# One core, attention gated with a state-space layer: the gate's store, the size of the state-product steps, the rule for zero products, and the order of head and tail

## The chip, the cores and the metric

The kernel runs on one core of one Trainium2 chip. The metric is the device time of one execution in microseconds (us); the times given are medians of several runs. TensorE (PE) multiplies matrices into PSUM, VectorE (DVE) and ScalarE (ACT) work element by element, GpSimd (POOL) does a few fills here, and SyncE (SP) issues nearly all DMA transfers, in the order of its own queue.

## The reference

x is 2048 x 512 in bf16. Two branches read it, and a gate mixes them:

```python
g = sigmoid((x * gate_w).sum(-1, keepdims=True))
qkv = (x @ wqkv)                       # 32 heads of 16
p = softmax(q @ k.T * 16 ** -0.5)      # per head, 2048 x 2048
a = (p @ v) @ wo
dt = exp(log_dt); logdA = dt * (A_re + 1j * A_im); dB = dt * (B_re + 1j * B_im)
K = einsum("dn,dnl,dn->dl", C, exp(logdA * l), dB).real    # l = 0 .. 2047, N = 128
b = causal_convolution(x, K) + x * Dskip                   # per channel, by FFT
out = g * a + (1 - g) * b
```

The attention has 32 x 2048 x 2048 exponentials. The convolution is computed in the kernel as a chunked recurrence: chunks of 64 positions, a state per channel carried from chunk to chunk by a scan, and inside each chunk a triangular product.

## The kernel before

**Attention.** The work is cut into 2048 tiles: 32 blocks (a query range of 512 and eight heads taken in two halves) by 16 key ranges of 128 by 4 heads of a block. A tile is 128 keys by 512 queries. Four tiles of one block and key range make a quad. Tiles go through in 683 groups of three. For each group TensorE makes the scores (`qk`, line 886) into one of two PSUM buffers SC0 and SC1, ScalarE takes the exponential of the whole group in one instruction (`ex`, line 901, recorded at line 905) into a ring ET of 15 slots, and `pv` (line 932) multiplies a quad of ET by V into the PSUM buffer OA. After the 16 quads of a block VectorE transposes OA (`norm_a`, line 974), divides by the sums (`norm_b`) and transposes back (`norm_c`). Score products of group g + 1 need the buffer that the exponential of group g - 1 has read.

**Tiles on VectorE.** Some groups give one of their three tiles to VectorE, which replaces the exponential by integer arithmetic on bf16 bits: `bits` (line 937) writes a tile of DZ, and when four tiles of a set are there, `batch` (line 947) makes two shifted variants (line 952) and TensorE adds three products per tile, against V and two scaled copies VS0 and VS1 of V. ScalarE's exponential of such a group covers two tiles. Which groups do so is decided in `decide` (line 795): a window of group numbers (`WIN`: first, last, number of buffers, how many sets of keys) must allow it, a buffer must be free, and VectorE's idle time, as the plan counts it, must have grown by a threshold `DVQ` that depends on the stage reached (the last S block, the first scan, the second scan done).

**State-space branch.** VectorE computes the parameters, then tables of powers (`table`, line 1204, into PT); PT is stored to DRAM by SyncE (line 1237) and read back transposed as Qt and as Py. From Qt and blocks of x TensorE makes the S products: `sstage` (line 1281), 16 blocks of four banks of 16 matmuls of 64 x 128 x 32, evicted by VectorE (line 1302). Two scans on VectorE (line 1310) of 30 steps each carry the states. `ystage` (line 1377) then makes 32 units of outputs, scaled by 1 - g from the tile gt, sent to DRAM and read back transposed as Yl. `kstage` (line 1258) makes the kernel inside a chunk. S, K and y products, projections, gate and output rows all share one PSUM bank, MB, under a lock.

**Gate.** `gate` (line 1455) makes 64 small products once all projections are done, an exponential on ScalarE, and then g and 1 - g as 128 x 16 floats, where row p and column i stand for position 128 i + p. They are needed in two other orders (gq and gt), so both are written to DRAM (lines 1479 and 1481) with the position running fastest, that is, as single floats, and read back by eight DMAs (lines 1485 and 1487).

**Order.** All engines' instruction streams are written out ahead by a planner in the same file. Each piece of work is a thread that yields (engine, cost, priority) and then records instructions; `Sched.fill` (line 367) runs, after each group, those threads that can start before the planned end of the exponential, on TensorE up to `OVER` past it. Costs are constants given with each instruction (`c=`). The planned costs fix only the order; on the chip the engines wait on semaphores.

**Zero products.** To keep TensorE's clock up, the planner adds products of zeros (`zero`, line 880). Work is counted in columns of a full 128 x 128 product of 512 (`a=`). After each group it asks for `FILL` columns per 1.335 us of planned ScalarE time, plus what was lacking before, less what was done, and fills up with zeros into OA or MB. `REST` and `FILL2` exist, but with the values given they do nothing.

**Head and tail.** Before the first group (from line 1612) x is transposed on TensorE and copied to xT, the first projections are made, and ScalarE takes exp(log_dt) and two sines, with the loads of its function tables between. After the last group (from line 1714) four groups of output products (a product with the identity that adds Yl, and four with Wo) go to MB and three banks of an SC buffer; the first three products with Wo can be made before the last block is normalised, the fourth needs it. Two copies on ScalarE and two on VectorE, and four stores end the kernel. Every instruction on TensorE is recorded in the helper `mm` (line 622), so all of them carry line 624.

## Time and profile before

| | us |
|---|---|
| median of 3 runs | 855.75 (854.38 to 861.9) |
| profiled execution, whole | 854.42 |
| its span, first to last instruction | 852.6 |
| ScalarE busy | 829.1 |
| VectorE busy | 775.1 |
| TensorE busy | 750.6 |
| exponentials (line 905), busy | 820.8 |

TensorE's mean granted clock is 0.994 of full speed. "Busy" is the time in which at least one instruction of an engine runs; matmuls and exponentials overlap their neighbours, so the distance from one to the next is shorter than a duration. In the rows of groups, the columns are line, engine, operation, output and inputs by name, shape, count; then busy time and the mean of one in ns; then the engine's idle time before them and what ended it. A name with a q (SPq, ACTq) is an engine's queue that issues DMAs. In tables of stretches each row has start and end, then the time, then busy time and count of TensorE, its weight loads, VectorE, ScalarE and GpSimd, then the granted clock, the DMA engines' share and GB/s. A chain row has start, time and what it was.

### The profile page before, as it was taken

How to read it: one execution, taken by the hardware profiler on the slowest of the kernel's cores; microseconds unless marked ns; L12 is line 12 of the kernel's file. 1: busy time of each engine (PE TensorE's matmuls, PEld its weight loads, DVE VectorE, ACT ScalarE, POOL GpSimd, SP SyncE). 2: the span in 40 equal slices, each digit the busy share in tenths (PEclk: the TensorE clock that was granted, in tenths of full speed). 3: DMA queues.
4: the chain of work that ended last, by engine and by line, in shares of the span. 5: the costliest groups of instructions: out<-in, count | busy, mean ns of one | idle time of the engine just before them, and what ended most of it. 6: DMA issues, size and time to landing. Idle time of an engine off the chain costs nothing.

```text
span 852.6 us, 23406 instructions
## 1 busy us (share of the span) xinstructions
PE 750.6 (88%) x10256; PEld 294.3 (35%) x10256; DVE 775.1 (91%) x1313; ACT 829.1 (97%) x695; POOL 11.0 (1%) x13
## 2 busy tenths in 40 slices
PE   7888888878758999999999999988889889999986
PEld 3232332222212443434442445334343233343322
DVE  5799999999959999998899999999999988997985
ACT  7999999999979999999999999999999999999995
POOL 4000000000000000000000000000000000000000
PEclk9999999999989999999999999999999999999999
DMA  9400102942733386558481568016575325454113
GB/s 204 121 2 10 35 4 103 172 153 95 60 129 149 61 191 174 87 146 142 72 109 21 103 100 150 2 49 142 149 160 140 102 88 121 102 137 116 31 35 100
DMA packets 209526, 86.66 MB, mean 102 GB/s; under 512 B 184208, under 2 KB 196368, under 8 KB 207376
## 3 DMA queue, kind: packets, MB, share of 16 engines
q1 hardware_dynamic: 207408, 83.99, 44.9%
q8 instruction: 80, 1.31, 0.6%
q10 hardware_dynamic: 2016, 1.18, 0.6%
q14 instruction: 22, 0.18, 0.1%
HBM read 35.17 MB, written 30.82 MB: 77 GB/s over the span
## 4 chain that ended last, share of the span: by engine, by line
ACT 78%; PE 18%; DMA 2%; DVE 1%; ACTq 0%; issue 0%; SPq 0%; DVEq 0%
ACT ET L905 78%; PE OA L624 7%; PE SC L624 6%; PE MB L624 6%; DMA gm_ptd<-PT 1%; DMA Wq<-in_A_wqkv_dram 1%; DVE tt L999 0%; ACTq L628 0%; DVE Kst L1270 0%; DVE OT L976 0%; ACT fo L1741 0%; DVE KT L714 0%; DVE PT L999 0%; DVE DZ L941 0%; ACT e L1074 0%
## 5 line engine op out<-in xcount | busy, mean ns | idle before, releaser
L905 ACT ACTIVATE ET<-SC 128x1536 bf16<-128x1536 f32 (+1 forms) x683 | 820.8, 1512 | 10.0 <-PE SC L624 9.3
L624 PE MATMUL SC<-Qm,KT 32*128 32x512 bf16 x2048 | 274.7, 385 | 78.1 <-ACT ET L905 63.7
L624 PE MATMUL OA<-wm 128*32 128x512 bf16 (+3 forms) x2136 | 248.0, 339 | 1.2 <-DVE wm L677 1.2
L624 PE MATMUL OA<-ET,VE 128*32 128x512 bf16 x1812 | 181.3, 392 | 6.5 <-DVE OT L976 6.0
L941 DVE TENSOR_SCALAR DZ<-SC 128x512 uint16<-128x512 f32 x236 | 157.4, 685 | 17.0 <-PE SC L624 15.3
L624 PEld LDWEIGHTS SC<-Qm,KT 32*128 32x128 bf16 x2048 | 70.6, 91 | 291.7 <-ACT ET L905 240.4
L624 PEld LDWEIGHTS OA<-ET,VE 128*32 128x32 bf16 x1812 | 46.3, 93 | 108.8 <-issue 99.3
L624 PEld LDWEIGHTS OA<-wm 128*32 128x32 bf16 (+2 forms) x2136 | 71.4, 95 | 32.8 <-issue 16.1
L624 PE MATMUL MB<-X,Qt 64*128 64x32 bf16 x1024 | 74.8, 231 | 0.0
L624 PEld LDWEIGHTS MB<-X,Qt 64*128 64x128 bf16 x1024 | 57.7, 109 | 25.3 <-issue 23.2
L1302 DVE TENSOR_SCALAR SG<-MB 128x512 bf16<-128x512 f32 x64 | 44.0, 688 | 7.8 <-PE MB L624 6.7
L952 DVE TENSOR_SCALAR DZ<-DZ 128x2048 uint16<-128x2048 uint16 x59 | 40.6, 688 | 8.4 <-PE OA L624 8.3
L1337 DVE TENSOR_TENSOR G<-s,s 128x512 f32<-128x512 f32 x60 | 41.3, 688 | 1.1
L1329 DVE TENSOR_TENSOR s<-G,MU 128x512 f32<-128x512 f32 x60 | 41.0, 684 | 0.0
L1334 DVE TENSOR_TENSOR s<-s,SG 128x512 f32<-128x512 f32 x60 | 41.0, 683 | 0.0
L1331 DVE TENSOR_TENSOR s<-G,MU 128x512 f32<-128x512 f32 x60 | 41.0, 683 | 0.0
L952 DVE TENSOR_SCALAR DU<-DZ 128x2048 uint16<-128x2048 uint16 x59 | 40.4, 688 | 0.6
L999 DVE TENSOR_TENSOR ft<-FP,L 128x1024 f32<-128x1024 f32 (+1 forms) x32 | 34.4, 1084 | 0.1
L999 DVE TENSOR_TENSOR PT<-tt,tt 128x1024 bf16<-128x1024 bf16 x48 | 32.9, 685 | 0.7
L624 PEld LDWEIGHTS MB<-Py,SG 128*32 128x32 bf16 x1024 | 29.6, 165 | 7.4 <-issue 4.1
L624 PE MATMUL MB<-Py,SG 128*32 128x64 bf16 x1024 | 30.1, 229 | 0.0
L976 DVE STREAM_TRANSPOSE OT<-OA 128x512 f32<-128x512 f32 x32 | 22.8, 711 | 4.2 <-PE OA L624 3.6
(166 smaller groups left out, 618.2 us busy)
## 6 DMA issues: line engine op xcount, KB each, us to landing
gm_ptd<-PT SPq DMA_DIRECT2D x16, 1024.0 KB, 5.9
Py<-gm_ptd SPq DMA_DIRECT2D x32, 512.0 KB, 4.4
gm_kpd<-Kst SPq DMA_DIRECT2D x16, 256.0 KB, 3.7
Tt<-gm_kpd SPq DMA_DIRECT2D x128, 32.0 KB, 3.4
gm_xrd<-in_A_x_dram SPq DMA_DIRECT2D x1, 2048.0 KB, 13.2
X<-gm_xrd SPq DMA_DIRECT2D x8, 256.0 KB, 4.7
Wo<-in_A_wo_dram SPq DMA_DIRECT2D x4, 512.0 KB, 4.1
XY<-gm_xrd SPq DMA_DIRECT2D x8, 256.0 KB, 4.2
```

Source lines behind the costliest of these rows:

```text
L624: op("PE", lambda t: t.matmul(out(), lhsT(), rhs(), start=start, stop=stop, skip_group_check=True, **kw), R, W, c=c, lat=.15, a=a, cfg=cfg)
L905: op("ACT", lambda a: a.activation(ET(512 * e, [[1, 512 * n]]), sc(0, [[1, 512 * n]]), AF.Exp, scale=DH ** -0.5), [(sc, i, g) for i in ran ...
L941: op("DVE", lambda v: v.tensor_scalar(z.u16(512 * k, [[1, 512 * n]]), sc(512 * na, [[1, 512 * n]]), XS, XB, ALU.mult, ALU.add), [(sc, na + ...
L952: op("DVE", lambda v: v.tensor_scalar(t.u16(0, [[1, 2048]]), z.u16(0, [[1, 2048]]), float(STEP[k][0]), None, ALU.add), R, W, c=.07 + 2048 ...
L976: op("DVE", lambda v: v.transpose(OT(512 * w, [[1, 512]]), OA(0, [[1, 512]])), [(OA, 0, b)], [(OT, w, b)], c=.64)
L999: op(eng, lambda v: v.tensor_tensor(o(), a(), b_(), f), R, W, c=c)
L1302: op("DVE", lambda v, bank=bank, par=par, part=part: v.tensor_scalar(sg(2 * SGH + SGH * part + CB * k8 + 16 * par, [[2 * SGH, 32], [1, 16] ...
L1329: op(e, lambda v: v.tensor_tensor(s2(0, W), G(0, W), MU(d0, [[0, 2], [1, 256]]), ALU.mult), key("G", "MU"), [(s2, 0)], c=F5)
L1331: op(e, lambda v: v.tensor_tensor(s3(0, W), G(256, [[-256, 2], [1, 256]]), MU(D + d0, [[D, 2], [1, 256]]), ALU.mult), key("G", "MU") + [(M ...
L1334: op(e, lambda v, so=so: v.tensor_tensor(s2(0, W), s2(0, W), sg(so, [[SGH, 2], [1, 256]]), ALU.add), [(s2, 0)] + ks, [(s2, 0)], c=F5)
L1337: op(e, lambda v: v.tensor_tensor(G(0, [[1, 512]]), s2(0, [[1, 512]]), s3(0, [[1, 512]]), ALU.add), [(s2, 0), (s3, 0)], [(G, 0)], c=F5)
```

## The change

- **Gate.** g and 1 - g now stand side by side in one tile of 32 columns. VectorE transposes it in 32 x 32 blocks into gT, whose rows hold 32 consecutive positions, and one DMA stores it in runs of 32 floats. The reads are as before, from the new places.
- **S products** go in steps of four instead of eight, with a planned cost of 0.058 instead of 0.035 each, and may begin at group 170 instead of 195. Other planned costs (V, Kst, AO, VS, y products) change too, and Yst has four buffers.
- **Windows.** `WIN`, `VSAT` and `DVQ` have other numbers: the last window begins at 620 with four buffers.
- **Zeros.** The planner keeps a list of TensorE's work with its planned start. After each group it sums the work that began no earlier than 3 us before the planned end of the exponential, and fills up to 3500 columns. `OVER` goes from 0.3 to 0.6.
- **Head.** Wq is loaded before Wk, ldt through SyncE's queue instead of ScalarE's, exp(log_dt) stands first on ScalarE, which takes a second of the four copies of xT, and TensorE gets four more products of zeros.
- **Tail.** The first group of output products becomes a thread of the lowest priority within the main loop, the last `pv` comes before the other groups, the fourth group comes after the first two closing products, and ScalarE issues one store instead of two.

```diff
-FILL = 1600
-FILL2 = 1600
-OVER = .3
-REST = (14, 0, 1792, 425)
+FILL = 3500
+HWIN = 3.0
+OVER = .6
-SGAT = (195, 260)
-SMM = .035
+SGAT = (170, 260)
+SMM = .058
-VSAT = (168, 600)
-WIN = ((180, 430, 2, 1), (430, 640, 2, 1), (640, 678, 3, 2))
-DVQ = (("scan1", 0.2), ("scan0", 0.8), ("S15", 2.0), (None, 0.7))
+VSAT = (158, 580)
+WIN = ((170, 475, 2, 1), (475, 620, 2, 1), (620, 678, 4, 2))
+DVQ = (("scan1", 0.2), ("scan0", 1.2), ("S15", 2.5), (None, 0.7))
...
         self.act += a
+        if a:
+            self.hist.append((self.tm[eng], a))
...
-    sb("Yst", 2 * 256)
+    sb("Yst", 4 * 256)
...
-    load("ACT", B["ldt"], lambda: dap(ins["ldt"], 0, [[0, P], [1, D]]), [(B["ldt"], 0)], [[1, D]])
+    load_w("Wq", 0, 0, P, 0)
     load_w("Wk", D, 0, P, 0)
-    load_w("Wq", 0, 0, P, 0)
+    load("SP", B["ldt"], lambda: dap(ins["ldt"], 0, [[0, P], [1, D]]), [(B["ldt"], 0)], [[1, D]])
...
-            for k0 in range(0, 16, 8):
-                yield ("PE", 8 * SMM)
-                for k in range(k0, k0 + 8):
+            for k0 in range(0, 16, 4):
+                yield ("PE", 4 * SMM)
+                for k in range(k0, k0 + 4):
...
-        op("DVE", lambda v: v.tensor_scalar(g1(0, [[1, 16]]), g(0, [[1, 16]]), -1.0, 1.0, ALU.mult, ALU.add), key("g"), key("g1"), c=.17)
+        op("DVE", lambda v: v.tensor_scalar(g(16, [[1, 16]]), g(0, [[1, 16]]), -1.0, 1.0, ALU.mult, ALU.add), key("g"), [(g, 1)], c=.17)
+        op("DVE", lambda v: v.transpose(gT(0, [[1, 32]]), g(0, [[1, 32]])), key("g") + [(g, 1)], key("gT"), c=.17)
         sch.mark("gp")
-        yield ("SP", .7, 1)
-        dma("SP", lambda e: e.dma_start(B["gd"].dram(0, [[1, P], [P, 16]]), g1(0, [[1, 16]]), allow_slow_non_contiguous=True),
-            key("g1"), [(B["gd"], 0)], c=.7, lat=9)
-        dma("SP", lambda e: e.dma_start(B["gd"].dram(S, [[1, P], [P, 16]]), g(0, [[1, 16]]), allow_slow_non_contiguous=True),
-            key("g"), [(B["gd"], 1)], c=.7, lat=9)
+        yield ("SP", .6, 1)
+        dma("SP", lambda e: e.dma_start(B["gd"].dram(0, [[32, 4], [P, 32], [1, 32]]), gT(0, [[1, 32]])), key("gT"), [(B["gd"], 0)], c=.6, lat=3)
...
+    op("ACT", lambda a: a.activation(B["dt"](0, [[1, D]]), B["ldt"](0, [[1, D]]), AF.Exp), key("ldt"), key("dt"), c=.6)
     for q4 in range(4):
...
-        if q4 == 1:
+        if q4 % 2:
...
-    op("ACT", lambda a: a.activation(B["dt"](0, [[1, D]]), B["ldt"](0, [[1, D]]), AF.Exp), key("ldt"), key("dt"), c=.6)
+    for k in range(4):
+        mm(lambda: OA(0, [[1, 512]]), lambda: wm(0, [[1, 128]]), lambda: wm(0, [[1, 512]]), [(wm, 0)], [(OA, 0, "warm")])
...
+    def ahead_of(i):
+        ident(i)
+        for pi in range(3):
+            out_mm(12 + i, banks[i], pi, -1)
+
+    def first():
+        yield ("AFTER", "outs")
+        yield ("AFTER", "c29")
+        yield ("LOCK", "MB")
+        yield ("PE", MM)
+        ident(0)
+        for pi in range(3):
+            yield ("PE", MM)
+            out_mm(12, banks[0], pi, -1)
...
-            lack += p.act
             qk(g + 1)
...
-        want = (FILL if g < REST[3] else FILL2) * (t - t0) / 1.335 + min(max(lack, -256), 768)
-        t0 = t
-        sch.rest = g < REST[3] and g % REST[0] < REST[1]
-        if sch.rest:
-            want = max(want, REST[2])
+        p.hist = [h for h in p.hist if h[0] >= t - HWIN]
+        want = max(0, FILL - sum(h[1] for h in p.hist) + p.act)
         sch.fill(t, t + OVER, want)
...
-    ahead_of(0)
+    pv(ends[31])
     ahead_of(1)
-    pv(ends[31])
     ahead_of(2)
-    ahead_of(3)
     norm_a(31)
     norm_b(31)
     for k in range(2):
         norm_c(31, k, 2)
         for i in (2 * k, 2 * k + 1):
             out_mm(12 + i, banks[i], 3, -1)
+        if k == 0:
+            ahead_of(3)
...
-        out_dma(12 + i, "ACT" if i in (0, 2) else "SP")
+        out_dma(12 + i, "ACT" if i == 2 else "SP")
```

More of the change, by code (lines that the diff above doesn't have):

```diff
@@ L99, in __init__ @@
         self.act = 0
+        self.hist = []
         self.cfg = None
@@ L285, in __init__ @@
         self.n = 0
-        self.rest = False
     def add(self, gen, prio):
@@ L374, in fill @@
                 if t.eng == "PE":
-                    if self.rest and t.prio in (2, 5):
-                        continue
                     own = sum(a[2].get("a", 0) for a in t.seg if isinstance(a, tuple))
@@ L455, in declare @@
     sb("ge", 16, FP32)
-    sb("g", 16, FP32)
+    sb("g", 32, FP32)
+    sb("gT", 32, FP32)
     sb("gq", 16, FP32)
-    sb("g1", 16, FP32)
     sb("Dpb", 16)
@@ L724, in vproj_ev @@
                                           MB(0, [[128, 4], [16, 8], [1, 16]])),
-           [(MB, 0, ('p', "V", pi, kq))], [(VE, (pi, 4 * kq + i)) for i in range(4)], c=.66)
+           [(MB, 0, ('p', "V", pi, kq))], [(VE, (pi, 4 * kq + i)) for i in range(4)], c=.61)
     def mk_qm(b, j):
@@ L928, in vscaled @@
                                                                            VE(pi * 4 * VG + kts[0] * VW, [[VG, len(kts)], [1, VSW]]), f, None, ALU.mult),
-                   [(VE, (pi, x)) for x in range(16)], [(VS[k], (step, pi))], c=.23)
+                   [(VE, (pi, x)) for x in range(16)], [(VS[k], (step, pi))], c=.23 if len(kts) == 4 else .3)
         sch.mark(f"VS{k}")
@@ L1268, in kstage @@
                    [(MB, 0, ('K', blk))], part == 0, part == 1, pos=(0, 32 * a), c=QUAD if a == 0 else 0, a=128, cfg="C")
-        yield ("DVE", .9, -1)
+        yield ("DVE", .8, -1)
         op("DVE", lambda v: v.tensor_copy(Kst(1024 * (blk % 2) + 63, [[P, 8], [1, T]]), MB(0, [[T, 8], [1, T]])), [(MB, 0, ('K', blk)), (Kst, "z")], [(Kst, blk % 2, blk)], c=.65)
         op("DVE", lambda v: v.tensor_scalar(Kst(1024 * (blk % 2) + 63, [[P, 8]]), MB(0, [[T, 8]]), B["Dp"](blk, [[1, 1]]), None, ALU.add),
-           [(MB, 0, ('K', blk)), (B["Dp"], 0)], [(Kst, blk % 2, blk)], c=.25)
+           [(MB, 0, ('K', blk)), (B["Dp"], 0)], [(Kst, blk % 2, blk)], c=.145)
         sch.unlock("MB")
@@ L1455, in gate @@
     def gate():
-        gp, ge, g, g1, gwT = (B[n] for n in ("gp", "ge", "g", "g1", "gwT"))
+        gp, ge, g, gT, gwT = (B[n] for n in ("gp", "ge", "g", "gT", "gwT"))
         yield ("DVE", .2)
@@ L1644, in record, with ident @@
     sch.mark("qm0")
+    o = SC[(NG - 2) % 2]
+    banks = [(MB, 0, 0), (o, 0, 0), (o, 512, 1), (o, 1024, 2)]
+    def ident(i):
+        b, off, sl = banks[i]
+        lt = 12 + i
+        mm(lambda: b(off, NAT), lambda: idb(0, [[1, P]]), lambda: Yl(lt * D, PERM), [(idb, 0)] + [(Yl, x) for x in range(NBLK)],
+           [(b, sl, ('o', lt))], True, False)
+    def ahead_of(i):
[11 more added lines that the diff above has]
+            out_mm(12, banks[0], pi, -1)
     def bases():
@@ L1650, in record @@
     for th, pr in ((norms(), 0), (qms(), 0), (projs(), 1), (gate(), .8), (ystage(), 2), (yloads(), 4), (params(), 2), (vscaled(0), 2.2), (vscaled(1), 2.2), (scan(), 3),
-                   (bases(), BP), (table(), 2), (ublocks(), 4), (xyloads(), 4), (early(), 1.5), (reload(), 5), (outs(), 6)):
+                   (bases(), BP), (table(), 2), (ublocks(), 4), (xyloads(), 4), (early(), 1.5), (reload(), 5), (outs(), 6), (first(), 6)):
         sch.add(th, pr)
@@ L1660, in record @@
     ring = {}
-    lack = t0 = bare = 0
+    lack = bare = 0
     for g in range(NG):
```

29 lines of the change are left out of this document (10 added, 19 removed).

## The prediction

> **What bounds the kernel now.** I read the page's busy shares and groups kept apart by shape first, then the chain that ended last, then the same groups inside two stretches.
>
> ```profile
> L905 ACT ACTIVATE ET<-SC 128x1536 bf16<-128x1536 f32 x446 | 609.0, 1699 | 7.9 <-PE SC L624 7.6
> L905 ACT ACTIVATE ET<-SC 128x1024 bf16<-128x1024 f32 x237 | 230.2, 1159 | 2.1 <-PE SC L624 1.7
> L941 DVE TENSOR_SCALAR DZ<-SC 128x512 uint16<-128x512 f32 x236 | 157.4, 685 | 17.0 <-PE SC L624 15.3
> L952 DVE TENSOR_SCALAR DZ<-DZ 128x2048 uint16<-128x2048 uint16 x59 | 40.6, 688 | 8.4 <-PE OA L624 8.3
> L952 DVE TENSOR_SCALAR DU<-DZ 128x2048 uint16<-128x2048 uint16 x59 | 40.4, 688 | 0.6
> ...
> 15.55 194.73 ACT ET L905 x145
> 519.71 322.23 ACT ET L905 x284
> ```
>
> ScalarE's exponentials are the clock of this kernel: 446 of three tiles, 237 of two. Their durations overlap, so I take the distance from one to the next. The chain has 145 back to back, all of three tiles (the first two-tile group comes later): 194.73/145 = 1.343 us. A two-tile one follows from the late stretch:
>
> ```profile
> L905 ACT ACTIVATE ET<-SC 128x1536 bf16<-128x1536 f32 x127 | 173.9, 1490 | 1.7 <-PE SC L624 1.6
> L905 ACT ACTIVATE ET<-SC 128x1024 bf16<-128x1024 f32 x96 | 93.3, 1062 | 2.1 <-PE SC L624 1.7
> ...
> L905 ACT ACTIVATE ET<-SC 128x1536 bf16<-128x1536 f32 x144 | 199.6, 1645 | 0.2 <-PE SC L624 0.2
> L905 ACT ACTIVATE ET<-SC 128x1024 bf16<-128x1024 f32 x141 | 136.9, 1225 | 0.0
> ...
> 256.00:520.00 264.00, 253.90 (x3327) 108.70 (x3323) 247.16 (x415) 260.73 (x223) 1.05 (x2) 1.00 0.58 115
> 520.00:842.00 322.00, 289.04 (x4695) 116.18 (x4699) 296.52 (x508) 322.00 (x285) 0.00 (x0) 1.00 0.43 101
> ```
>
> The first pair is 256 to 520 us, the second 520 to 842; the last two rows give TensorE, weight loads, VectorE and ScalarE busy. Late: (322 - 144 x 1.343)/141 = 0.912 us. So a set of four tiles taken by VectorE saves ScalarE 4 x (1.343 - 0.912) = 1.72 us and costs VectorE 4 x 0.685 + 2 x 0.688 = 4.1 us. From 256 to 520 the exponentials need 127 x 1.343 + 96 x 0.912 = 258.1 of 264 us: 5.9 us are lost there, with TensorE busy 96%. The rest of the loss is one hole, the first part of the change.
>
> **The gate's store.** SyncE's queue, the waits of 205 to 262 us, and TensorE's clock:
>
> ```profile
> 212.69 3.96 SPq L1481 DMA_DIRECT2D gm_gd<-g  x1
> ...
> 235.25 0.32 SPq L1485 DMA_DIRECT2D gq<-gm_gd  x1
> ...
> 239.14 0.90 SPq L1237 DMA_DIRECT2D gm_ptd<-PT  x2
> ...
> SPq L1485 <- DMA gm_gd<-g: 10.7, 1, 10.7
> ...
> DVE PT L1220 <- DMA gm_ptd<-PT: 7.4, 2, 3.9
> ...
> ACT ET L905 <- PE SC L624: 6.2, 2, 5.6
> PE OA L624 <- DVE OT L976: 6.0, 1, 6.0
> ...
> 233.18 0.69 DVE L999 TENSOR_TENSOR PT<-tt,tt 128x1024 bf16<-128x1024 bf16 x1
> 247.55 0.43 DVE L1220 COPY PT<-B 128x1024 bf16<-128x1024 bf16 x1 [3.86 <-DMA gm_ptd<-PT]
> 251.15 0.71 DVE L976 STREAM_TRANSPOSE OT<-OA 128x512 f32<-128x512 f32 x1
> ...
> 250.20:253.60 3.40, 1.69 (x15) 0.41 (x15) 3.37 (x7) 0.00 (x0) 0.00 (x0) 0.50 0.00 0
> 711.00:714.40 3.40, 2.51 (x50) 1.12 (x46) 2.68 (x5) 3.40 (x4) 0.00 (x0) 1.00 0.23 44
> gm_ptd<-PT SPq DMA_DIRECT2D x16, 1024.0 KB, 5.9
> gm_ytd<-Yst SPq DMA_DIRECT2D x32, 64.0 KB, 2.9
> ```
>
> Two writes of 2048 single floats each, the second issued at 212.7, are not there until 235. SyncE stands 10.7 us before the first read of them (L1485), and behind it in its queue stands the store of PT, whose last product was done at 233.9 but which is issued at 239.14. VectorE waits 7.4 us to overwrite PT; queued behind that copy is the transpose of OA (251.15), TensorE waits for that 6.0 us, and ScalarE stands 5.6 us, then 0.6 us more while TensorE runs at half clock: 6.2 us.
>
> After: 128 rows of 32 floats, 128 bytes each, in one DMA, and one VectorE transpose in front, which finds cover in the 7.4 us that VectorE waits here; without cover it costs one small operation. No such store of the gate is in this trace; the nearest row is Yst's, runs of 64 bf16, the same 128 bytes, four times as many: 2.9 us. Bounds: 0 and the 22 us of now; I take 2.9. Then PT's store goes out at about 234 and is done some 5.9 us later, at 240; OA's transpose, 3.6 us behind the copy (251.15 - 247.55), comes near 244, before the 246 at which TensorE now stops (it goes on when the transpose ends, at 251.9, after 6.0 us). Next late would be the eight reads of the gate that stand ahead of PT's store on SyncE, four of L1485 at 0.32 us and four like it; they now come before 234. Gain **6.2** us; bounds 4 and 6.8.
>
> [...]
>
> **The tail.** Now (chain and order of time):
>
> ```profile
> 842.81 0.98 PE MB L624 x4
> 843.78 0.87 PE SC L624 x4
> ...
> 844.59 0.40 PE L624 MATMUL OA<-ET,VE 128*32 128x512 bf16 x4
> 845.04 0.72 DVE L976 STREAM_TRANSPOSE OT<-OA 128x512 f32<-128x512 f32 x1 [2.87 <-PE OA L624]
> ...
> 847.48 0.81 PE L624 MATMUL SC<-Wo,OnT 128*128 128x512 bf16 x3
> 847.97 1.29 DVE L1743 CAST fo<-SC 128x512 bf16<-128x512 f32 x2 [0.44 <-PE SC L624]
> 848.68 0.94 SPq L1502 DMA_DIRECT2D out_dram<-fo  x2
> ```
>
> The last PV stands behind two groups of output products, 0.98 + 0.87 = 1.85 us; the change puts it first. The next two groups fit under the 2.4 us in which VectorE normalises. The fourth, 0.87 us, comes between the second and third closing product: the last product ends at 849.16 instead of 848.29, the last copy starts about 0.6 us later, and SyncE now issues three stores (0.47 us each) instead of two, ScalarE one. I give back 0.75: gain **1.1** us. The first group becomes a thread of the lowest priority, which takes the shared bank once the last reloaded rows are out; from then zeros have only OA to go to. It has ScalarE's last exponentials as cover; without a free place it runs behind them and costs its 0.98. Bounds 0 and 1.85.
>
> **The head.**
>
> ```profile
> 2.26 6.24 DMA Wq<-in_A_wqkv_dram
> ...
> 6.10 0.59 ACT L1622 CAST xT<-SC 128x512 bf16<-128x512 f32 x1 [1.98 <-PE SC L624]
> 6.58 0.63 ACT L1625 ACTIVATE dt<-ldt 128x512 bf16<-128x512 bf16 x1
> ...
> 9.90 1.28 ACT L905 ACT_TABLE_LOAD   x1
> ...
> 11.23 0.41 PE SC L624 x3
> 11.67 1.45 ACT ET L905
> ```
>
> Wq is issued a place earlier on ScalarE's queue, so the first scores could be ready up to 1 us sooner (one place is about half of that, and ldt's place is freed too). ldt's load goes to the front of SyncE's queue and sets back AimT and all behind it by one issue; AimT is read only together with dt, and the loads behind it are for later groups. But ScalarE takes a second copy of xT (one follows the other after 0.48 us), so its two table loads slide: 9.90 + 0.48 + 1.28 = 11.66. Gain **0.1**; bounds 0.6 either way. The four extra products on TensorE lie in its wait for Wq and xT.
>
> **S products, zeros, OVER.** S products come in pieces of four instead of eight, at a planned price of 0.058 us instead of 0.035, and may start from group 170 instead of 195. Smaller pieces at a higher price are put only where more of TensorE is free, so fewer should push the next scores back: of the 5.9 us lost I take back **3**, half; bounds 0 and 5.9. Where they start earlier, their 64 evictions meet VectorE's tables, which are then late by as much; that is in the bounds of the sets. Zeros: 1600 columns per 1.335 us becomes 3500 per 3.0 us or, as the window reaches up to 0.6 us ahead, 3.6: 1199 to between 1167 and 972 per us. I cost that at nothing, hidden by TensorE's idle share; a fall of the clock is a rival.
>
> **Sets.** VectorE stands idle 322 - 296.5 = 25.5 us after 520, some of it in waits for TensorE. The changed windows (four buffers from group 620, the seven keys of a block earlier) allow more sets there, the higher thresholds during the scans allow fewer. No row shows the result: between -2 and +4 sets, +3.4 and -6.9 us; I take one more, **1.7** us. Four Yst buffers instead of two, the scaled copies of V made earlier and the other planned costs (Kst, V, AO, y products) change no instruction's duration; they move work within the plan, and stand in these bounds.
>
> **Sum.** 6.2 + 1.1 + 0.1 + 3 + 1.7 = 12.1 us. The profiled execution took 854.42 us: 842.3. The median of the runs shown is 1.3 us above it: **843** us, own range 835 to 848.
>
> **Rivals.**
> Only the hole and the tail: sets and S products bring nothing. 843 + 4.7 = 848. For it: VectorE is 92 to 94% busy in both stretches, and a plan that moves its work may only move the loss. Chance 0.2.
>
> The wider reach, slower: TensorE's work may be placed up to 0.6 us past the end of an exponential instead of 0.3. Scores must start 0.44 us ahead of their exponential (11.23 to 11.67), so a two-tile group leaves 0.912 - 0.44 = 0.47: work that fills the reach makes ScalarE 0.13 us late. Three-tile groups leave 0.9. In all 237 groups it is 31 us; it eats the whole gain from 93 groups, and makes the kernel over 1% slower from about 160; with 200 of them 26 us, 869. For it: TensorE 96% busy from 256 to 520. Against: 90% after, where ScalarE loses 0.2 us. Chance 0.12, with a middle price of 18 us: 861.
>
> Falls of the clock: with thinner zeros TensorE drops to half speed. The row at 250.2 shows 3.4 us at half speed; a fall of twice that length puts TensorE 3.4 us back, and in the stretch at 96% ScalarE with it; three make 853. Against: from 711 to 714.4 TensorE was busy 2.51 of 3.4 us and kept 1.00; the only low clock follows a stop of 6 us. Chance 0.1. [...]
>
> The store stays slow (short runs still late): 849, chance 0.04. My forecast: 0.54.
>
> **How the numbers follow.** A measurement of this kernel can tell about 1%: 847.2 to 864.3 is no change. Faster by over 1%: nearly all of the forecast, 0.51, two fifths of the first rival, and a share of the clock's: 0.64. Slower: part of the reach's rival, and plans worse than I can see: 0.11. Same: 0.25. The range, 834 to 856, leaves out the reach's rival and four or more extra sets.
>
> **What would show it.** SyncE's wait at the gate's reads under 1 us, no ScalarE hole near 246, clock 1.00 throughout; the last PV 0.5 us after the last exponential; first exponential at 11.6; from 256 to 520 under 4 us lost; more than 237 two-tile exponentials. It is wrong if two-tile groups come fewer, if their distance exceeds 0.95 us, or if the clock's digits dip in several slices.

## The result, and the profile after

| | before | after |
|---|---|---|
| median of 19 executions each, same chip, us | 855.72 (854.06 to 861.9) | 848.76 (843.19 to 854.72) |
| ratio, with its 95% interval | | 0.9923 (0.99 to 0.9945) |
| profiled execution, us | 854.42 | 852.25 |
| its span, us | 852.6 | 850.5 |
| its mean granted clock | 0.994 | 0.978 |

The change gains 7 us, 0.8%: less than the 1% that I had named as the bound, and less than the 12 us forecast. The executions of the changed kernel lie 11.5 us apart, and they follow TensorE's clock: 843.19 and 843.65 us at a mean clock of 0.996, 854.17 and 854.2 us at 0.976 and 0.977; the slowest, 854.72 us, is at 0.982. The profiled execution is one of the slower ones. The ratios in this document leave out executions more than 1.5% above the fastest of their kernel (below, one of `ldt_back_again` and three of `steps_of_eight`); the medians count all.

The page of the changed kernel, the span in 40 slices, one digit each (9 is 90% or more):

```profile
PE   7877777778788999999998999998898779999987
...
PEclk9999999999999987999999999999989999999999
```

PEclk, the granted clock, dips in the 15th, 16th and 30th slice; dips were the sign by which I said the forecast would fail. TensorE itself looks full in those slices (9s): from 311.0 to 331.5 us, at a clock of 0.50, it is busy 20.50 of 20.5 us with 182 matmuls, from 300 to 311, at 1.00, 9.47 of 11 us with 116. The groups:

```profile
L904 ACT ACTIVATE ET<-SC 128x1536 bf16<-128x1536 f32 x438 | 599.2, 1736 | 4.9 <-PE SC L623 4.8
L904 ACT ACTIVATE ET<-SC 128x1024 bf16<-128x1024 f32 x245 | 237.9, 1168 | 4.8 <-PE SC L623 3.3 <-PE OA L623 1.3
L940 DVE TENSOR_SCALAR DZ<-SC 128x512 uint16<-128x512 f32 x244 | 162.1, 683 | 19.8 <-PE SC L623 19.1
L951 DVE TENSOR_SCALAR DZ<-DZ 128x2048 uint16<-128x2048 uint16 x61 | 41.9, 687 | 8.4 <-PE OA L623 8.4
```

61 sets instead of 59, and 245 two-tile exponentials instead of 237. The stretches, in the columns used before (TensorE, weight loads, VectorE, ScalarE, GpSimd; granted clock; DMA):

```profile
242.00:250.00 8.00, 6.93 (x92) 2.43 (x84) 7.47 (x14) 7.99 (x8) 0.00 (x0) 1.00 0.04 9
300.00:311.00 11.00, 9.47 (x116) 3.79 (x112) 9.66 (x19) 10.40 (x9) 0.00 (x0) 1.00 0.88 228
311.00:321.00 10.00, 10.00 (x93) 3.35 (x93) 7.66 (x13) 8.50 (x6) 0.00 (x0) 0.50 0.53 90
321.00:331.50 10.50, 10.50 (x93) 2.94 (x91) 7.90 (x13) 7.55 (x7) 0.00 (x0) 0.50 0.70 94
331.50:342.00 10.50, 9.84 (x126) 3.68 (x123) 9.61 (x19) 10.13 (x11) 0.00 (x0) 1.00 0.67 261
...
632.00:640.00 8.00, 7.97 (x108) 2.37 (x100) 7.15 (x13) 6.75 (x7) 0.00 (x0) 0.58 0.51 118
```

Where the hole was, ScalarE is busy 7.99 of 8 us. In its place stand 20.5 us at half clock from 311.0, in which ScalarE is idle 1.5 + 2.95 = 4.45 us. TensorE made no long stop before that fall: it was busy 9.47 of the 11 us ahead of it, and its longest pause there was 0.6 us.

**The account of the two profiled executions.** Back to back, one exponential follows the next after 1.331 us (three tiles) or 0.905 us (two) in both traces; what a distance has beyond that I call lost. Start of the first exponential: 11.67 to 14.12, +2.45. Eight more two-tile exponentials, 8 x (1.331 - 0.905): -3.4. Lost: 22.7 to 23.0, +0.3. From the start of the last exponential to the end: 11.04 to 9.51, -1.5. Sum -2.15, and the spans differ by 2.1. The +0.3 hides two large movements. In cold stretches, those at half clock, counted from one window of 3.4 us ahead of the fall to 1 us behind the rise, 6.6 us were lost before, all by the hole, and 12.3 after, in five stretches of 37.5 us together. Outside them the loss went from 16.1 to 10.7, and in 256 to 520 us alone from 9.3 to 3.3. (The 5.9 us that the prediction names there go by its larger distances, 1.343 and 0.912, and count the exponential that the window's edge cuts.) Where the edge of a cold stretch is drawn moves such a loss by up to 2 us.

### The profile page after: what moved, and what is told of

Read it like the earlier page. It is cut to its first block, busy times and chain, and to the rows that moved or that the text cites. A ratio compares the mean times of both kernels' runs of the same rounds, so it can differ in the third digit from the quotient of the medians.

```text
span 850.5 us, 22098 instructions
## 1 busy us (share of the span) xinstructions
PE 740.3 (87%) x9615; PEld 284.0 (33%) x9615; DVE 780.9 (92%) x1325; ACT 826.3 (97%) x696; POOL 11.0 (1%) x13
## 4 chain that ended last, share of the span: by engine, by line
ACT 84%; PE 9%; DVE 3%; DMA 3%; SPq 0%; issue 0%; DVEq 0%
ACT ET L904 83%; PE SC L623 4%; PE OA L623 3%; PE MB L623 2%; DMA gm_ptd<-PT 1%; DMA Tt<-gm_kpd 1%; DVE DZ L940 1%; DMA x0n<-in_A_x_dram 1%; DVE DZ L951 0%; SPq L1363 0%; DVE OT L975 0%; DVE SG L1301 0%; ACT L904 0%; ACT L1626 0%; DVE G L1336 0%
## 5 line engine op out<-in xcount | busy, mean ns | idle before, releaser
L623 PE MATMUL SC<-Qm,KT 32*128 32x512 bf16 x2048 | 278.3, 392 | 94.8 <-ACT ET L904 83.4
L623 PE MATMUL OA<-wm 128*32 128x512 bf16 (+3 forms) x1527 | 215.1, 364 | 1.2 <-DVE wm L676 1.2
L623 PE MATMUL OA<-ET,VE 128*32 128x512 bf16 x1804 | 184.1, 399 | 0.2 <-DVE OT L975 0.2
L940 DVE TENSOR_SCALAR DZ<-SC 128x512 uint16<-128x512 f32 x244 | 162.1, 683 | 19.8 <-PE SC L623 19.1
L623 PE MATMUL MB<-X,Qt 64*128 64x32 bf16 x1024 | 82.7, 230 | 0.0
L623 PEld LDWEIGHTS OA<-wm 128*32 128x32 bf16 (+2 forms) x1527 | 57.8, 95 | 26.5 <-issue 14.0
L623 PEld LDWEIGHTS MB<-Py,SG 128*32 128x32 bf16 x1024 | 27.0, 169 | 7.3 <-issue 5.1
L623 PE MATMUL MB<-Py,SG 128*32 128x64 bf16 x1024 | 28.3, 233 | 0.0
L1339 DVE CAST SG<-G 128x512 bf16<-128x512 f32 x60 | 25.4, 423 | 1.5
```

Source lines behind the costliest of these rows:

```text
L623: op("PE", lambda t: t.matmul(out(), lhsT(), rhs(), start=start, stop=stop, skip_group_check=True, **kw), R, W, c=c, lat=.15, a=a, cfg=cfg)
L940: op("DVE", lambda v: v.tensor_scalar(z.u16(512 * k, [[1, 512 * n]]), sc(512 * na, [[1, 512 * n]]), XS, XB, ALU.mult, ALU.add), [(sc, na + ...
L1339: op(e, lambda v, so=so: v.tensor_copy(sg(so, [[SGH, 2], [1, 256]]), G(0, W)), key("G"), ks if c < NCH - 2 else [(sg, k, (h, 'G')) for k i ...
```

## The experiments

Three theories were to be told apart. **Phase**: the clock falls after a stretch of a few us with little work in TensorE, on a grid of windows whose place against the kernel's start is another in each execution, so that the same kernel is caught in another place each time. (In the profiles of before and after any two changes of the granted clock lie a whole multiple of 3.413 us apart: the cold stretches last 6.83 us before, and 3.41, 20.48, 3.41, 6.83 and 3.41 us after; the grid begins 0.12 us past the span's start before, 0.38 us after.) **Place**: single known places starve TensorE and can be filled. **Head**: dt's logarithm, now loaded first on SyncE, holds up x. The edits work on the list of instructions that the planner has recorded, so that the order of all else stays; only `steps_of_eight` is planned anew. The zeros that are added or left out change no value of the output.

Since the time follows the clock, I also give, for each kernel, a straight line through time against clock over its executions, read at full clock (a number worked out; with 4 to 7 executions it is loose).

| kernel | executions | median, us | ratio to before | median clock | at full clock, us |
|---|---|---|---|---|---|
| before (on the three chips of the experiments) | 54 | 855.4 | | 0.991 | 850.9 |
| after | 19 | 848.76 | 0.9923 (0.99 to 0.9945) | 0.984 | 842.1 |
| gate_only | 10 | 850.8 | 0.9939 (0.9912 to 0.9967) | 0.993 | 848.9 |
| gate_thin | 7 | 849.2 | 0.9937 (0.9915 to 0.9959) | 0.995 | 846.3 |
| gate_thick | 5 | 851.34 | 0.9932 (0.9907 to 0.9957) | 0.994 | 848.7 |
| ldt_back | 7 | 850.34 | 0.9921 (0.9885 to 0.9956) | 0.982 | 840.9 |
| ldt_back_again | 12 | 850.06 | 0.9921 (0.9888 to 0.9954) | 0.981 | 838.2 |
| ldt_back_thick | 4 | 845.31 | 0.9891 (0.9857 to 0.9925) | 0.996 | 842.8 |
| thick_again | 6 | 848.82 | 0.991 (0.9881 to 0.9939) | 0.993 | 844.9 |
| thick_again_ldt_first | 6 | 850.04 | 0.9925 (0.99 to 0.995) | 0.995 | 849.2 |
| ldt_back_control | 4 | 844.19 | 0.9853 (0.9823 to 0.9882) | 0.993 | 842.1 |
| control_again | 6 | 843.09 | 0.9869 (0.9846 to 0.9892) | 0.994 | 841.3 |
| steps_of_eight | 12 | 852.81 | 0.996 (0.9935 to 0.9985) | 0.983 | 845.0 |

The slopes with many executions are 4.9 us for 0.01 of the clock (after) and 5.3 (before). By these lines the changed kernel is 8.8 us faster at equal clock, and gives part of it back because it holds 0.984 where before holds 0.991.

### The gate's store alone

`gate_only` is the kernel before in its own order, with the store of the change (in short form; the reads follow the new places):

```diff
-    dma SP  gd[0:S]  <- g1 as [[1, P], [P, 16]]        # 2048 single floats
-    dma SP  gd[S:2S] <- g  as [[1, P], [P, 16]]
+    DVE  gT <- transpose(g | 1 - g)
+    dma SP  gd <- gT as [[32, 4], [P, 32], [1, 32]]     # 128 runs of 32 floats
```

> The kernel before with the gate's store alone changed (transpose, one DMA in runs of 128 bytes), every other instruction in the order of before. My account: the hole near 246 us goes, SyncE's wait at the gate's reads falls from 10.7 us to under 3, the granted clock goes from 0.994 to about 1.00, and the time falls by 6 to 6.5 us, to about 849. Rival (short runs are still slow, or the loss only moves to another wait): under 2 us.

`gate_thin` leaves out four of every twelve zero products into OA besides:

```diff
+if f.__name__ == "op" and a[0] == "PE" and (bufs["wm"], 0) in a[2] and 0 <= q < 683 and a[3][0][0] is bufs["OA"]:
+    n += 1
+    if n % 12 >= 8:
+        continue
```

> As gate_only, in the same order, but 4 of every 12 zero products into OA are left out (they add zeros, so nothing computed is lost). If thinner zeros by themselves make TensorE's clock fall, the granted clock falls below 0.99, the times of single executions scatter by several us, and the median is 3 to 10 us above gate_only. If zeros only take TensorE's time and the falls come from something else in the change (S products earlier or in other steps), the clock stays at 1.00 and the time is that of gate_only or up to 2 us less.

`gate_thick` adds 7,000 columns of zeros to `gate_only` at its own thin places:

> gate_only with 7 thousand columns of zeros at its own thin places. It has neither the new sets nor the new S steps nor the new tail. If these are worth what the traces say (two sets 3.4, S stretch about 5, tail 1.2 us), it stays some 6 to 9 us above thick_again, near 850, at a clock of 0.995 or more. If the rest of the change brings nothing once the clock is held, it is equal to thick_again.

All three are faster than before by 0.6 to 0.7%, about 5 us, and in all three the hole is gone. The waits of `gate_only` from 205 to 262 us (who waited for whom; total, times, longest):

```profile
PEld SC L642 <- ACT ET L923: 29.6, 41, 1.0
PE SC L642 <- ACT ET L923: 12.0, 33, 0.6
...
DVE PT L1238 <- DMA gm_ptd<-PT: 0.5, 1, 0.5
```

VectorE's wait for the store of PT is 0.5 us where it was 7.4, and SyncE and ScalarE have no row; in `gate_thin` and `gate_thick` it is the same. Its lost time is 17.2 us against 22.7: the hole was worth 5.5 us, less than the 6.2 of the prediction, and its executions gain about that. That is less than the 6 to 6.5 us expected, and the clock is 0.991 in the profile where I expected 1.00. The profile gains only 3, because its head is 2.8 us longer:

```profile
8.00:18.30 10.30, 7.33 (x34) 3.18 (x36) 5.14 (x10) 6.66 (x9) 2.89 (x2) 0.50 1.13 262
```

The clock fell at 8.1 us and the first projections ran at half speed. The head's instructions are those of before, whose profile escaped that; so 11.67, the start that I forecast from, was a lucky one: in the other three profiles with the old head it is 14.50, 13.90 and 14.24 us.

`gate_thin` took the second way that I had named: a third fewer zeros into OA (1428 products in place of 2136, and the changed kernel has 1527) brought neither more falls nor more time. Neither did `gate_thick` gain by more zeros (7,424 columns). It was to stay 6 to 9 us above `thick_again` of the parts below, run on the same chip, and stays 2.5 above it; against `ldt_back_control`, also on that chip, it is 7.2. By these two the number of zeros decides little in the old plan; where they stand may.

### dt's logarithm first on SyncE

`ldt_back` is the changed kernel with that load again behind the first load of x on ScalarE's queue:

```diff
+f, q, (_, fn, R, W) = log.pop(3)               # the load of ldt
+log.insert(1, (f, q, ("ACT", fn, R, W)))       # behind that of x0n
```

> The changed kernel with one DMA moved: ldt's load is back on ScalarE's queue behind x0n, ahead of Wq; all engines' work in the order of the changed kernel. If ldt's load ahead of x0n is what holds up x0n, x0n lands near 4.6 us instead of 7.7, the first exponential starts at 11.5 to 12 instead of 14.1 us, and the time falls by about 2.4 us. If x0n's late landing is chance or comes from Wq's place, the first exponential stays near 14.

The head of the changed kernel, rows of the chain that ended last (start, time, what):

```profile
0.74 6.96 DMA x0n<-in_A_x_dram
7.71 0.05 issue
7.76 1.46 PE SC L623 x12
...
14.12 1.45 ACT ET L904
```

and the first transfers, x's in the kernel before, then both in `ldt_back` (KB, then us from issue to landing):

```profile
x0n<-in_A_x_dram ACTq DMA_DIRECT2D x1, 512.0 KB, 3.9
...
x0n<-in_A_x_dram ACTq DMA_DIRECT2D x1, 512.0 KB, 4.3
ldt<-in_B_log_dt_dram ACTq DMA_DIRECT2D x1, 128.0 KB, 5.4
```

With ldt first, x0n lands after 7.0 us, behind it after 4.3 (3.9 before); over all profiles it is 6.7 to 7.0 in three with ldt first and 3.9 to 4.3 in ten with it behind. ldt writes 128 KB by reading one row of 512 values 128 times; why x0n lands later beside it was not tried. In the six profiles of the new head with ldt behind, the first exponential starts at 11.7 to 12.6 us, in the three with ldt first at 13.1, 14.1 and 15.3. The old head's three cold starts were at 13.9 to 14.5: beside those the rest of the new head gains about 2 us, and the load takes it away again.

The 2.4 us expected do not show in the median of `ldt_back`, whose clock is 0.982. By the lines at full clock it is 1.2 us ahead of the changed kernel, `ldt_back_again` 3.9. A cleaner pair has more zeros in both (next part) and was run on one chip: `thick_again` with ldt behind, `thick_again_ldt_first` with it first.

> thick_again with ldt's load where the changed kernel has it, first on SyncE's queue. If it holds x0n up, x0n lands about 2.7 us later than in thick_again, the first exponential starts near 14 instead of 12.2, and the median is about 2 us higher. If that was chance, the two are equal.

848.82 and 850.04 us in the medians; in the executions at a clock of 1.000, 845.32 against 849.81 and 850.27. Its first exponential starts at 15.29, that of `thick_again` at 12.21:

```profile
0.74 6.70 DMA x0n<-in_A_x_dram
...
9.38 3.41 PE OA L642 x8
12.79 1.28 PE SC L642 x4
```

The last two rows show the rest: x came so late that TensorE's zeros (OA, 3.41 us for eight; 0.43 us each is the pace of half clock: `column_rates` below has 104 products in 44 us at 0.50) stand right in front of the projections. So the load makes x late, and the first exponential by some 2 us on average of the profiles. In the medians 1.2 us of the 2 expected show, less than their intervals tell apart.

### More zeros, at thin and at rich places

In `ldt_back_thick` 28,400 columns of zeros are added at 55 places where the trace of the changed kernel has thin windows and TensorE is idle; `thick_again` adds 10,000 more, 15 of its groups where it is not idle. `ldt_back_control` was meant as the control: 56 groups, 28,700 columns, at places whose windows are rich. A group is

```diff
+for j in range(4):      # w = 512 in most, 32 columns each, side by side
+    log.append((f, q, ("PE", lambda t, j=j, w=w: t.matmul(OA(0, [[1, w]], 32 * j, 32), wm(0, [[1, 32]]), wm(0, [[1, w]]),
+               start=False, stop=False, skip_group_check=True, tile_position=(0, 32 * j)), [(wm, 0)], [(OA, 0, b)])))
```

> As ldt_back, plus 56 groups of zero products (28 thousand columns, about 12 us of TensorE's time) put into places where the trace of the changed kernel shows TensorE idle and few columns done in the 3.4 us around. If thin stretches make the clock fall, the granted clock rises from about 0.985 to above 0.99, the scatter shrinks, and the median falls by 4 to 8 us against ldt_back. If the falls do not depend on zeros, the clock stays and the time is equal or up to 3 us worse.

> ldt_back_thick with another 10 thousand columns of zeros, put where the trace of ldt_back_thick still shows under 2900 columns in some stretch of 3.413 us, 15 of them at places where TensorE has no idle time. [...] If thick places are not what counts, falls stay as in ldt_back_thick or the forced zeros cost 2 us.

> ldt_back with 56 groups of zeros, 28.7 thousand columns, as many as in ldt_back_thick, but at idle places of TensorE where the columns around are already most (over 3300 in every stretch of 3.413 us). If the place counts and not the number, clock and scatter stay as in ldt_back (0.975 to 0.99, median near 850). If more zeros anywhere help, the clock rises above 0.99 and the median falls to about 845.

At the thin places the clock (0.996) and the 5 us against `ldt_back` came as expected; with still more zeros I expected 843 to 845 us and a fall or none, and 848.82 with two falls came. The control was the fastest of all: 844.19 us, ratio 0.9853, at a clock of 0.993, the second way that I had named for it. "Phase" said that it should do what `ldt_back` does. With 4 executions against 7 that could be luck, so both were run again beside each other:

> The load of dt's logarithm back behind the first load of x, as before, beside the zeros at rich places on the same chip. Theory (which thin windows lower the clock is a matter of the phase of a grid that runs freely): 844 to 851 again with a spread of its own, a clock of 0.978 to 0.995, and each 0.01 of the clock is worth 3 to 4.5 us. Rival (what the added zeros do counts): this one 3 us or more behind the other in the medians at equal clock too.

> The same with 56 groups of four zero products at places where TensorE's windows are rich. Theory: its thin windows are those of the kernel without them, so its falls come as often; more runs of it spread over 842 to 851 as the other's, median within 2 us of it. Rival: 842 to 844.5 in all runs, as in the four there are, because zeros at rich places take time from the planner's later groups or thicken windows beside them; then the median lies 3 us or more ahead.

850.06 us (841.2 to 854.16, 12 executions) against 843.09 (842.17 to 845.86, 6): my expectation, medians within 2 us, failed again. The 19 executions of `ldt_back` fall into two sorts, 7 from 841.2 to 846.2 us at a clock of 0.988 and more, 12 from 849.5 to 854.2 at 0.982 and less; the 10 of the control all have the times of the first sort, 842.0 to 845.9 us. The traces show what the second sort is; no profile of this order without added zeros is of the first. `ldt_back_again`:

```profile
300.00:310.00 10.00, 8.96 (x109) 3.63 (x102) 8.69 (x17) 9.09 (x9) 0.00 (x0) 1.00 0.92 189
310.00:320.00 10.00, 10.00 (x97) 3.31 (x93) 8.05 (x13) 7.96 (x7) 0.00 (x0) 0.51 0.48 80
320.00:330.00 10.00, 10.00 (x89) 2.82 (x86) 6.75 (x12) 7.88 (x7) 0.00 (x0) 0.50 0.81 134
330.00:337.60 7.60, 7.60 (x65) 2.13 (x61) 5.45 (x10) 5.42 (x6) 0.00 (x0) 0.50 0.61 255
```

and the same stretch of `control_again`:

```profile
298.00:308.00 10.00, 9.05 (x123) 3.76 (x115) 9.87 (x19) 9.94 (x10) 0.00 (x0) 1.00 0.94 234
308.00:318.00 10.00, 9.32 (x124) 3.83 (x121) 9.83 (x16) 10.00 (x8) 0.00 (x0) 1.00 0.54 89
```

All three profiles of this order without added zeros (after, `ldt_back`, `ldt_back_again`) fall at 309.5 to 311.0 us and stay cold for 20.5 to 27.3 us; neither profile with the control's zeros does. 20.5 us at half clock take 0.012 off the mean clock of 850 us, about the distance between the two sorts, and in these three stretches ScalarE loses 6.7, 6.7 and 8.6 us, about the distance in time. By the lines at full clock `ldt_back_again` is not behind (838.2 against 841.3): what the zeros change is the clock. Ahead of the fall, the timeline of VectorE in `ldt_back_again` and then in `control_again`:

```profile
302.33 0.42 DVE L1221 COPY PT<-B 128x1024 bf16<-128x1024 bf16 x1
303.98 0.43 DVE L1221 COPY PT<-B 128x1024 bf16<-128x1024 bf16 x1 [1.22 <-DMA gm_ptd<-PT]
305.52 0.68 DVE L942 TENSOR_SCALAR DZ<-SC 128x512 uint16<-128x512 f32 x1
```

```profile
301.50 0.76 DVE L1238 COPY PT<-B 128x1024 bf16<-128x1024 bf16 x2
303.38 0.68 DVE L959 TENSOR_SCALAR DZ<-SC 128x512 uint16<-128x512 f32 x1
```

The second copy into PT waits 1.22 us for the store of its old content, with the same wait, 1.2 us, in the other two profiles that fall, and with none in the five of this plan that have zeros added. The tile behind it reads its SC buffer later, and TensorE's scores wait for that, 0.4 us in `ldt_back` and `ldt_back_again`; counted as in the last part of this section, the window ahead of the fall holds 2170 to 2590 columns, the thinnest there in the control's two profiles 2890 and 2970. That the late store is the cause is read from this agreement; no run moves it alone. So there is a place as well as a phase. In `ldt_back` that store takes 8.2 us to land, in `control_again` 6.3; which of the 56 groups makes the difference, and how, stays open.

At the thin places the zeros do what was asked of them: one fall in the profile of `ldt_back_thick`, two in `thick_again`. But they seem to cost time. Lost outside cold stretches are 15.1 and 16.3 us (19.9 in `thick_again_ldt_first`, which has no fall), against 10.8 and 13.6 in `ldt_back` and its repetition, 13.4 and 12.3 with the control's zeros. A likely reason, which no run shows by itself, is that a thin place is thin because TensorE waits there for its next work, and zeros set in front of that work delay it: in 296 to 312 us VectorE waits 1.3 us for scores in both profiles, and not at all with the control's zeros. `control_again` beats both kernels: 11 to 12 us below before, and some 5 us below the changed kernel by the ratios, 0.9869 (0.9846 to 0.9892) against 0.9923 (0.99 to 0.9945), measured on two chips.

### S products in steps of eight

`steps_of_eight` is the changed kernel with one loop as before, planned anew:

```diff
-            for k0 in range(0, 16, 4):
-                yield ("PE", 4 * SMM)
-                for k in range(k0, k0 + 4):
+            for k0 in range(0, 16, 8):
+                yield ("PE", 8 * SMM)
+                for k in range(k0, k0 + 8):
```

> The changed kernel with only the S products back in steps of eight; the order is planned anew, which leaves 63 sets of VectorE tiles in place of 61. Theory (steps of four are what brought ScalarE's lost time in 256 to 520 us, outside the cold stretches, from 8.4 us to 2.7): it is 7 to 9 us again here; with two sets more, worth 3.4 us less of exponentials, it ends 1 to 4 us behind the changed kernel at equal clock. Rival (the wider reach, or the hole's end, brought it): the lost time stays at 2 to 4 us and it ends about 3 us ahead at equal clock.

Its ratio is 0.996 (0.9935 to 0.9985), above the changed kernel's 0.9923, though the intervals just overlap and the chips differ. Three of its 12 executions took 862.5 to 864.2 us at a clock of 0.952 to 0.962; the line at full clock gives 845.0 with them and 842.8 without, against 842.1. So it is not shown to be behind at equal clock, and its two additional sets make its exponentials 3.4 us shorter:

```profile
L904 ACT ACTIVATE ET<-SC 128x1536 bf16<-128x1536 f32 x430 | 586.5, 1738 | 7.5 <-PE SC L623 4.2 <-PE OA L623 2.7
L904 ACT ACTIVATE ET<-SC 128x1024 bf16<-128x1024 f32 x253 | 243.8, 1143 | 5.4 <-PE OA L623 2.6 <-PE SC L623 2.4
```

In 256 to 520 us, outside cold stretches, 5.9 us are lost, between the 3.3 of the changed kernel and the 9.3 of before. So by one profile of each the steps of four, with the order that they bring, account for 2.6 of the 6.0 us; the other 3.4 come from the rest of the new plan (reach, zeros, start at 170), not taken apart further. My 7 to 9 us expected here were too many.

### What lowers the clock, by itself

`column_rates` leaves the whole computation out (its operands and output are zeros; one execution). TensorE alone runs 128 matmuls, 512 wide, of one shape, then 80 of the full array, then the next shape; at the end full matmuls that each wait for a ScalarE copy. In short form:

```diff
+for rows, cols in STAGES:
+    for k in range(80):  matmul(OA, wm[:128, :128], wm[:128, :512])
+    for k in range(128): matmul(OA[:cols], wm[:rows, :cols], wm[:rows, :512])
+for n in (512, 640, 768, 896):
+    for k in range(80):  matmul(OA, wm[:128, :128], wm[:128, :512])
+    for k in range(40):  copy(a, wz[:, :n]); matmul(OA, wm[:128, :128], a[:, :512])
```

> This kernel leaves the whole computation out and only measures TensorE's clock: fifteen stages, each 80 matmuls of the full array (128 rows, 128 columns, 512 wide) and then 128 of the same width with fewer rows (32, 36, 40, 42, 44, 46, 48, 52, 64 with 128 columns) or fewer columns (32, 40, 42, 44, 48, 64 with 128 rows); then four stages in which 40 full matmuls each wait for a ScalarE copy of 512, 640, 768 and 896 elements. [...] Rival (only idle time of TensorE lets the clock fall): it holds in all fifteen, and in the stages with waits too, whose pauses are under 1 us. Second rival (rows in use are counted in steps of 32, or only rows or only columns count): the turn lies at 32 rows, or in one of the two series alone.

Groups (rows x columns of the weights behind the names) and, below, four stretches: 48 rows; 52 rows; 32 columns of 128 rows; waits for copies of 640 elements:

```profile
L616 PE MATMUL OA<-wm 48*128 48x512 bf16 x128 | 50.3, 585 | 0.0
...
L616 PE MATMUL OA<-wm 32*128 32x512 bf16 x128 | 49.6, 578 | 0.0
...
L616 PE MATMUL OA<-wm 128*32 128x512 bf16 x128 | 27.8, 379 | 0.0
L616 PE MATMUL OA<-wm 52*128 52x512 bf16 x128 | 27.8, 376 | 0.0
```

```profile
440.00:484.00 44.00, 44.00 (x104) 14.73 (x103) 0.00 (x0) 0.00 (x0) 0.00 (x0) 0.50 0.00 0
504.00:531.00 27.00, 27.00 (x126) 11.75 (x125) 0.00 (x0) 0.00 (x0) 0.00 (x0) 1.00 0.00 1
594.00:621.00 27.00, 27.00 (x126) 12.12 (x125) 0.00 (x0) 0.00 (x0) 0.00 (x0) 1.00 0.00 1
...
908.00:922.00 14.00, 13.54 (x23) 2.40 (x23) 0.00 (x0) 14.00 (x23) 0.00 (x0) 0.50 0.00 0
```

In each of the seven stages with 32 to 48 rows the 128 products take 49.1 to 50.4 us, in the two with 52 and 64 rows and the six with 32 to 64 columns of 128 rows 27.8. The stretch with 48 rows is at a clock of 0.50 with TensorE busy 44.00 of 44 us, those with 52 rows and with 32 columns are at 1.00, busy 27.00 of 27. The rival "only idle time counts" is dead. So is my own count by the share of the array, rows and columns alike: in this run the clock goes with the **rows in use** and not with the columns, and the turn that I expected at 42 to 44 rows lies between 48 and 52. At full clock a product of 512 columns follows the last after 0.216 us (128 with 52 rows in 27.8 us, each 0.376 us long), so that 3.413 us, the step of the granted clock in the profiles of before and after, hold some 8090; 48 rows are 0.375 x 8090 = 3030 columns' worth and fell, 52 rows are 3290 and held.

In this kernel most narrow products run four side by side (in `after` four of 32 rows take 0.40 us together from 302.55, four of 32 columns 0.40 us from 302.87), so that counting them by their share of the array comes near to the rows in use. Counted so, over the twelve profiles of the change and its variants from 20 to 835 us: of some 2700 windows at full clock with 3000 columns or more, none is followed by a fall; of the few dozen with 2700 to 3000 a small part is; of 20 to 30 with fewer, most. There are 27 falls in all. A window's edge cuts matmuls in two, so single windows are uncertain by some 200 columns.

## Why the prediction was right or wrong

- **Time and range.** 848.76 against 843 (842.3 and 1.3 are 843.6), inside 834 to 856, but short of the 1% that I gave 0.64. That it came so near is in part luck, two errors of opposite sign. In the account of the two profiles the parts of my sum gave more than its 12.1 us: 6.6 by the hole, 5.4 elsewhere outside cold stretches, 3.4 by the sets and 1.5 by the tail, less 2.45 by the head, are 14.5. The falls of the clock, which the sum put at nothing, took 12.3 of it back.
- **The hole: right**, 6.2 in size a little high against the 5.5 us of the experiment. SyncE issues PT's store at 233.22 at once, and ScalarE is busy 7.99 of the 8 us from 242. The eight reads come before 222, as the step wanted. The store of 128-byte runs holds nothing up here: no row waits for it.

```profile
208.70 1.01 SPq L1479 DMA_DIRECT2D gm_gd<-gT  x1
...
221.29 0.48 SPq L1484 DMA_DIRECT2D gt<-gm_gd  x1
233.22 0.83 SPq L1236 DMA_DIRECT2D gm_ptd<-PT  x2
```

- **The tail: right.** 1.1 forecast; 11.04 to 9.51 is 1.5, against the 10.4 to 10.5 of the three gate kernels 0.9 to 1.0. The last PV comes half a microsecond ahead of its transpose, with the second and third group behind it, and VectorE waits for it 0.73 us in place of 2.87:

```profile
842.23 0.39 PE L623 MATMUL OA<-ET,VE 128*32 128x512 bf16 x4
842.55 0.40 PE L623 MATMUL SC<-Yl,idb 128*128 128x512 bf16 x1
842.67 0.72 DVE L975 STREAM_TRANSPOSE OT<-OA 128x512 f32<-128x512 f32 x1 [0.73 <-PE OA L623]
```

- **The head: wrong.** I forecast 0.1 gained, bounds 0.6 either way; the first exponential came 2.45 us later, some 2 us of it by ldt's load. The step that failed: "ldt's load goes to the front of SyncE's queue and sets back AimT and all behind it by one issue". I followed the move through the queue it enters and not through the transfers that run at the same time, and x0n's landing went from 3.9 to 7.0 us. Nor did I see that one profile's 11.67 was not what the old head does in the three others, 13.9 to 14.5; beside those the changed head, 14.12, neither gains nor loses.
- **S products: right in kind, too small in size.** 3 us forecast, 6.0 taken back outside cold stretches; only 2.6 of them go with the steps of four, which is the mechanism that I had named.
- **Sets: right in sign.** One more forecast (1.7 us), two more came (3.4).
- **Zeros at no cost: wrong, and the step that decides.** "I cost that at nothing, hidden by TensorE's idle share; a fall of the clock is a rival." The rival came, at a chance of 0.1 and with "three make 853": the profile has five cold stretches and took 852.25. What I set against it, one stretch busy 2.51 of 3.4 us that kept 1.00, was read by busy time and without the grid: it holds some 2520 columns, but the grid of that trace cuts it into parts of two windows of 3590 and 3770. In `gate_only` the same three exponentials fall into one window, 707.81 to 711.23, busy 2.47 us with some 2600 columns, and the clock falls behind it. The price was wrong as well: I reckoned a fall as 6.8 us long and 3.4 us dear. The fall at 310 us lasts 20.5 to 27.3 us and costs ScalarE 6.7 to 8.6. At half clock the windows of that stretch count 2200 to 3020 columns and the clock stays at 0.50; it rises behind one of 3060 to 3460. Still, as far as `gate_thin` tells, it isn't the thinner zeros as such, but the place of the work in the new plan, above all at 310 us.
- **The wider reach as a rival: not seen.** Outside cold stretches the changed kernel lost less from 256 to 520, and back to back its two-tile groups follow after 0.905 us.

## What to carry to other kernels

Judge filler work and thin stretches by the rows of the array in use per 3.413 us, worst case over every place of that grid, not by TensorE's busy share: here the clock held with 52 of 128 rows and fell with 48, TensorE busy throughout, and none of some 2700 windows with 3000 columns or more was followed by a fall. Look first at the places where another engine's wait makes TensorE late, since the fall at one of them lasted 20.5 to 27.3 us; filling where TensorE is just about to get its work may have cost part of what it saved (15.1 and 16.3 us lost outside cold stretches, against 10.8 and 13.6 without such zeros). When a load is moved to another queue, check what lands later beside it (x0n: 7.0 us instead of 4.3), and take a starting time from more than one execution (the old head: 11.67 us in one profile, 13.9 to 14.5 in three).

## What the runs showed of the hardware that was not expected

- In `column_rates` the clock fell without idle time: with 48 of 128 rows in use it was 0.50 and TensorE busy 44.00 of 44 us, with 52 rows 1.00, and with 32 of 128 columns 1.00 as well.
- With short waits the turn lay close to that in the same run: full matmuls that wait for copies of 512 elements, one every 0.52 us or some 3360 columns in 3.413 us, were at a clock of 1.00 (866 to 882 us); with copies of 640, one every 0.63 us or some 2770, it was 0.50 (908 to 922), and 0.50 with 768 (948 to 975).
- In the three profiles in which ldt's load, which reads one 1 KB row 128 times, comes first on SyncE's queue, x0n, issued at the same time on ScalarE's, landed after 6.7 to 7.0 us; in the six of the new head with ldt behind x0n after 4.2 to 4.3. Which feature of the load does so was not tried.
- An added 28,700 columns of zeros at places already full of work made the kernel 7 us faster in the median (843.09 against 850.06 us); the traces point to one stretch that no longer falls, and which of the groups keeps it up is open.
